# Quarter-tile masks, a first K load in four pieces, zero products at the start, fewer K copies and seven x buffers in a fused attention and mixture kernel

## The chip, the cores and the metric

The kernel runs on 1 core of one Trainium2 chip. The metric is the time of one execution on the device in microseconds (us). Before the change three executions took 289.18, 290.21 and 291.86 us; the median, 290.21 us, is the time to beat. A separate execution was profiled: it took 289.33 us, and its trace spans 287.5 us.

Engines are named as the profile names them: PE does the matrix products (PEld its weight loads), DVE and ACT are the vector and the activation engine, POOL does memory copies and small vector work here, SP issues every DMA transfer.

## The reference, cut to what matters

```
# attention: B=2, H=8, S=768, D=64; window |i-j| < 16 and 24 block summaries
scores_l = scale * q @ k.T ; masked to the window
scores_s = scale * q @ k_sum.T + log(32)      # k_sum: max over blocks of 32 keys
a = softmax(concat(scores_l, scores_s)) ; attn = a @ concat(v, v_sum)   # v_sum: block means
x = attn as [1536, 512]
h = x @ w_in [512, 2048] ; g = h * tanh(softplus(h)) ; y = g @ w_out [2048, 512]
# soft mixture: 8 experts, 4 slots each, D=512, F=1024
logits = y @ phi ; d = softmax over tokens ; slot_input = d.T @ y
slot_out[e] = relu(slot_input[e] @ w1[e]) @ w2[e]
out = softmax over slots(logits) @ slot_out
```

## The kernel before, in words

The 1536 rows are worked through as twelve tiles t = 0..11 of 128 rows, six to a batch. A tile's attention holds 8 heads and two windows of 64 queries. For each window the 120 score columns are 96 window keys and 24 block summaries. PE forms the scores of a tile as 16 products of 64 by 64 by 120 (task `S`, L419), four at a time on the quarters of its array. For t = 0..4 the mask is added on PE by products of `spread_sb` and `mask_sb` that open the accumulation (L414): two products of 128 rows and 480 columns for an inner tile, four on half the columns of the array for an edge tile. For t = 5 and later DVE adds it (`masked`, L434). Then DVE takes the row maximum (`red`, L427), ACT the exponential (L441), DVE or POOL normalizes (`nm`, L456), PE transposes (`AT`, L462), and PE multiplies with V (`AV`, L472) into `x`.

Of `w_in` there are four blocks of 512 columns, fb = 0..3. Each is loaded in two halves of 1 MB through three staging slots (8, 9, 10), and each half is decoded by one ACT pass (L487) and two DVE passes (L488, then L489, which frees the staging slot for the next load). The decoded block is scaled and split in two half-precision planes: the high one by ACT (L518), the low one by DVE (L519, two to a block). Tile 0 uses the decoded block at once in full precision (`H32`, L611); from t = 1 each x is split in two planes too, and `H` is 48 products per tile (L617 to L619). `w_out` comes through the same staging slots. ACT evaluates the activation with `Mish` (L625), which needs another function table than the exponential, so that ACT reloads a table (`ACT_TABLE_LOAD`) at each turn between the two.

The mixture's routing runs beside this, tile by tile (L679 to L770). The 33 expert loads, 16 of `w1` and 17 of `w2` (L848), go into big slots as these come free. The tail is the experts' two products (L915, L967) and the output.

What sets the order: a table `ORDER` of task numbers, `CHOICE` of engines and `SLOT` of buffers. Each engine executes its tasks in that order and stalls on semaphores. All transfers stand in one order on SP, and a transfer that has to wait holds up those behind it.

The names that the change touches: `mask_sb` and `spread_sb` are the mask's two factors; `kb` is K by head, and `kh` is K already cut into windows. In batch 0, K comes as two `kb` loads of 768 KB; DVE reduces each to block maxima (L319), POOL copies these into the K buffer (`kplace`, L372) and cuts the windows of t = 0..5 out of the loaded K (`kwin`, L354 to L360). In batch 1 only t = 6 and 7 are cut on chip; t = 8..11 load `kh`. `x_b` are five x buffers, three in slot 20 and two in slot 21: tile t takes one of slot 21 when t % 5 > 2, that is t = 3, 4, 8, 9. Slot 21 becomes free for an expert load when the last `H` of those tiles is done. `warm` is a new task, `busy` (L664) an old one of the same kind at the end.

Of the kernel before, what the change touches and what calls it, by code (L numbers as in the profile page):

```python
# [21 lines left out]
NT = B * S // 128  # L22
# [78 lines left out]
    ],  # L101
    "POOL": [
        196, 199, 203, 222, 229, 243, 246, 250, 253, 267, 270, 274, 277, 291, 294, 298, 301, 317, 323, 366,
        388, 407, 413, 426, 432, 445, 451,
    ],
}
# [973 lines left out]
```

## Time and profile before

| what | value |
|---|---|
| median of three executions | 290.21 us (289.18 to 291.86) |
| profiled execution | 289.33 us, span 287.5 us |
| PE busy | 268.0 us of the span (93%) |
| DVE, ACT, POOL busy | 195.0, 207.8, 52.2 us |
| moved by DMA | 80.58 MB, mean 280 GB/s |

A busy time says how long an engine had an instruction in work. Start times count from the start of the span. In a timeline row the bracket at the end tells how long the engine stood idle before the row and which instruction let it go on. The clock column (PEclk) is the share of full clock granted to PE; half of it is the lower of its two levels, 1.2 in place of 2.4 GHz.

### The profile page before, as it was taken

To read this page: it belongs to the slowest core of one execution; us is meant where nothing else is said; L and a number is where in the kernel's file an instruction comes from. 1 tells how busy PE (TensorE), PEld (TensorE's weight loads), DVE (VectorE), ACT (ScalarE), POOL (GpSimd) and SP (SyncE) were. 2 spreads that over 40 slices of the span, in tenths; PEclk is the share of its full clock that TensorE was granted. 3 is DMA by queue.
4 is the path that set the end of the run, shared out by engine and by line. 5 is a ranking of instruction groups with operands and counts; after the bars stand their busy time and mean duration, and the time that the engine had idled before them with its cause. 6 is when DMAs were issued, how large, how long until landed. Compare 5 with 4: busy or idle time off the path is not lost.

```text
span 287.5 us, 7828 instructions
## 1 busy us (share of the span) xinstructions
PE 268.0 (93%) x3144; PEld 151.4 (53%) x3144; DVE 195.0 (68%) x460; ACT 207.8 (72%) x488; POOL 52.2 (18%) x91
## 2 busy tenths in 40 slices
PE   0889879999999999999999999999999998999997
PEld 0557445555456564565556545455645743234475
DVE  2489899999999898778659667686523575002352
ACT  1297889979988879999969999899459653003232
POOL 1559225430070531001211111000000010100000
PEclk9997999999999999999999999999999999999999
DMA  7999999599999879999695677989988999999997
GB/s 253 415 358 344 358 339 365 137 335 308 317 246 315 154 107 222 205 241 223 241 192 128 76 222 141 299 157 210 325 317 313 370 388 314 412 423 421 423 346 252
DMA packets 58467, 80.58 MB, mean 280 GB/s; under 512 B 44352, under 2 KB 47936, under 8 KB 53824
## 3 DMA queue, kind: packets, MB, share of 16 engines
q1 hardware_dynamic: 58432, 80.10, 91.3%
q8 instruction: 24, 0.39, 0.5%
q14 instruction: 11, 0.09, 0.1%
HBM read 66.46 MB, written 3.15 MB: 242 GB/s over the span
## 4 chain that ended last, share of the span: by engine, by line
PE 44%; DVE 20%; DMA 16%; ACT 14%; issue 5%; POOL 1%; SPq 0%; DVEq 0%; ACTq 0%; POOLq 0%
PE bank L617 8%; PE bank L619 7%; PE bank L618 7%; DMA slot<-w2b 6%; DVE slot L489 4%; ACT slot L441 4%; DMA slot<-w2a 3%; PE bank L754 2%; ACT slot L625 2%; DMA slot<-kb 2%; DMA slot<-wi 2%; PE bank L472 2%; DVE slot L488 2%; DMA slot<-wo 2%; ACT L625 2%
## 5 line engine op out<-in xcount | busy, mean ns | idle before, releaser
L617 PE MATMUL bank<-slot,slot 128*128 128x512 f16 x176 | 66.9, 380 | 0.7 <-ACT slot L625 0.7
L618 PE MATMUL bank<-slot,slot 128*128 128x512 f16 x176 | 66.7, 379 | 0.0
L619 PE MATMUL bank<-slot,slot 128*128 128x512 f16 x176 | 66.7, 379 | 0.0
L456 POOL TENSOR_TENSOR slot<-slot,sm 128x480 f32<-128x480 f32 x19 | 22.7, 1197 | 91.7 <-DVE sm L452 25.2
L625 ACT ACTIVATE slot<-bank,scal 128x512 f32<-128x512 f32 x44 | 29.2, 687 | 9.8 <-PE bank L619 6.7
L641 DVE SCALAR_TENSOR_TENSOR slot<-slot,sc,slot 128x512 f16<-128x512 f32 x40 | 30.6, 774 | 4.3 <-ACT slot L637 4.0
L619 PEld LDWEIGHTS <-slot 128*128 128x128 f16 x176 | 17.2, 98 | 21.0 <-DVE slot L480 0.3
L255 ACT COPY slot<-bank 120x512 f32<-120x512 f32 (+5 forms) x45 | 17.7, 430 | 14.3 <-PE bank L923 8.3
L617 PEld LDWEIGHTS <-slot 128*128 128x128 f16 x176 | 17.4, 99 | 16.8 <-issue 0.6
L625 ACT ACT_TABLE_LOAD x20 | 25.7, 1283 | 0.8 <-PE bank L619 0.4
L618 PEld LDWEIGHTS <-slot 128*128 128x128 f16 x176 | 17.2, 98 | 16.6 <-issue 1.5
L441 ACT ACTIVATE slot<-slot,sm 128x120 f32<-128x120 f32 x56 | 21.3, 383 | 0.6 <-DVE sm L435 0.5
L441 ACT ACTIVATE slot<-bank,sm 128x120 f32<-128x120 f32 x40 | 13.9, 369 | 10.5 <-POOL sm L431 10.5
L257 DVE COPY slot<-bank 128x256 f32<-128x256 f32 (+3 forms) x30 | 14.4, 513 | 9.8 <-PE bank L462 4.0
L489 DVE SCALAR_TENSOR_TENSOR slot<-slot,slot 128x1024 int32<-128x1024 int32 x16 | 20.4, 1277 | 0.3
L487 ACT ACTIVATE slot<-slot 128x1024 f32<-128x1024 f32 x16 | 18.6, 1172 | 1.8 <-DMA slot<-wi 1.4
L462 PE MATMUL bank<-ident_sb,slot 128*120 128x128 f32 x96 | 14.7, 278 | 2.1 <-POOL slot L456 1.3
L360 POOL COPY slot<-slot 128x192 f32<-128x192 f32 x26 | 13.8, 550 | 12.4 <-DMA slot<-kb 12.3
L967 PE MATMUL bank<-slot,slot 128*32 128x384 f32 (+1 forms) x256 | 15.2, 382 | 0.2 <-DMA slot<-w2b 0.2
L611 PE MATMUL bank<-slot,slot 128*128 128x512 f32 x32 | 15.4, 599 | 0.0
L472 PE MATMUL bank<-slot,slot 120*64 120x64 f32 x384 | 14.6, 233 | 0.5 <-ACT phi_sb L385 0.3
L419 PE MATMUL bank<-slot,slot 64*64 64x120 f32 x384 | 14.2, 289 | 0.6 <-POOL slot L372 0.6
(175 smaller groups left out, 478.4 us busy)
## 6 DMA issues: line engine op xcount, KB each, us to landing
slot<-w SPq DMA_DIRECT2D x16, 1024.0 KB, 5.5
slot<-w2a SPq DMA_DIRECT2D x12, 960.0 KB, 9.0
slot<-wi SPq DMA_DIRECT2D x8, 1024.0 KB, 6.8
slot<-wo SPq DMA_DIRECT2D x8, 1024.0 KB, 6.0
slot<-vh SPq DMA_DIRECT2D x12, 384.0 KB, 5.3
slot<-w2b SPq DMA_DIRECT2D x4, 1024.0 KB, 18.6
slot<-kb SPq DMA_DIRECT2D x4, 768.0 KB, 5.5
slot<-qh SPq DMA_DIRECT2D x12, 256.0 KB, 5.4
```

Of the source, the lines that this page charges most:

```text
L255: sca.copy(dst, src)
L441: sca.activation(A_b[ha.slot][:, hp], src, AF.Exp, bias=m[:, hp:hp + 1], scale=1.0 if late else 0.125, accum_out=m[:, 4 + hp:5 + hp])
L456: (pool if e == "POOL" else vec).tensor_tensor(A_b[ha.slot], A_b[ha.slot], sm_t[hq.slot][:, 4:8].unsqueeze(2).to_broadcast([128, 4, KW]), ...
L472: pe.matmul(banks[hm.slot][64 * r:64 * r + 64, 128 * hp + 64 * w:128 * hp + 64 * w + 64], Vb[i][:, w, c:c + 64], AT_b[hat2[r].slot][0:KW, ...
L487: d = add("ACT", ("dec_a%d" % n,) + name, lambda e: sca.activation(dst(), st(1).bitcast(F32), AF.Prelu, scale=2.0 ** -112, alpha=-(2.0 ** ...
L489: return add("DVE", ("dec_o%d" % n,) + name, lambda e: vec.scalar_tensor_tensor(di(), st(0), 29, di(), op0=ALU.logical_shift_right, op1=AL ...
L611: pe.matmul(banks[hb.slot], xf_b(hx.slot)[:, dc], slots[hw.slot][:, 512 * dc:512 * dc + 512], start=(dc == 0), stop=(dc == 3))
L617: pe.matmul(ps, x[:, 0, dc], w[:, 0, dc], start=(dc == 0), stop=False)
L618: pe.matmul(ps, x[:, 0, dc], w[:, 1, dc], start=False, stop=False)
L619: pe.matmul(ps, x[:, 1, dc], w[:, 0, dc], start=False, stop=(dc == 3))
L625: g_done[t, fb] = [add("ACT", ("mish", t, fb), lambda e, dst=dst, hb=hb, sc=sc: sca.activation(dst(), banks[hb.slot], AF.Mish, scale=sc), ...
L641: d = add("DVE", ("glo", t, fb), lambda e: vec.scalar_tensor_tensor(pv(1), g(), sfb[:, t // TB:t // TB + 1], pv(0), op0=ALU.mult, op1=ALU. ...
```

## The change

1. The masks become 64 by 64 quarters. `mask_sb`, `spread_sb` and a new `bias_sb` (the 24 summary columns) hold the same 64 rows in both halves of the partitions; each is loaded in two transfers. `add_mask` issues for each quarter one product of 96 columns a head and one of 24. A masked tile has eight such products in place of two or four. Every user waits for all six loads (`masks_in`).
2. The first K comes in four loads of 384 KB in place of two, each with its own DVE reduction. K sits in slots 4 and 5, no longer 6 and 7; the decoded blocks 2 and 3 change places with it.
3. `vsum` is zeroed by POOL at the start, and 22 products of zeros (`warm`) are chained on PE.
4. Windows of K are cut on chip for t = 0..3 and 6, 7; t = 4 and 5 load `kh`.
5. There are seven x buffers: slot 21 holds four, for t = 3, 4, 5, 6, 10, 11.
6. `ORDER`, `CHOICE` and `SLOT` are new.

```diff
@@ masks and zero products
-    L_spread = add("DMA", ("ld_spread",), lambda e: dma(out=spread_sb, in_=spread))
-    L_mask = add("DMA", ("ld_mask",), lambda e: dma(out=mask_sb, in_=masks.rearrange("k p n -> p k n")))
+    L_spread, L_mask = None, None
+    for w in range(2):
+        L_spread = add("DMA", ("ld_spread", w), lambda e, w=w: dma(out=spread_sb[HALF[w]].rearrange("p (a m) -> p a m", a=2), in_=spread.rearrange("(a p) m -> p a m", a=2)[:, :, 0:64]), after=[L_spread])
+        L_mask = add("DMA", ("ld_mask", w), lambda e, w=w: dma(out=mask_sb[HALF[w]], in_=masks[:, 0:64].rearrange("k p n -> p k n")), after=[L_mask])
+        L_bias = add("DMA", ("ld_bias", w), lambda e, w=w: dma(out=bias_sb[HALF[w]], in_=masks[0, 64:128, 96:KW]), after=[L_mask])
+    L_mask = join(("masks_in",), [t for t in pl.tasks if t["name"][0] in ("ld_spread", "ld_mask", "ld_bias")])
+    def add_mask(ps, r, w, of, stop):
+        a, at = ps.shape[1], (64 * r, 64 * w)
+        for stat, mov, cols in ((slice(0, 64), mask_sb[HALF[r], of, 0:96], slice(0, 96)), (slice(64, 128), bias_sb[HALF[r]], slice(96, KW))):
+            pe.matmul(ps[HALF[w], :, cols], spread_sb[HALF[r], stat], mov.unsqueeze(1).to_broadcast([64, a, cols.stop - cols.start]), start=cols.start == 0, stop=stop and cols.start > 0, tile_position=at)
+    Z_w = add("POOL", ("fillw",), lambda e: pool.memset(vsum, 0.0))
+    for j in range(22):
+        warm.append(add("PE", ("warm", j), lambda e: pe.matmul(banks[hwarm.slot][:, 0:480], zeros[:, 0:128], zeros[:, 0:480], start=True, stop=True), [warm[-1]], acq=[] if j else [hwarm], use=[hwarm] if j else []))
@@ scores
-                for rows, of in () if late else [(slice(0, 128), 1)] if kind == 1 else [(slice(0, 64), min(kind, 1)), (slice(64, 128), max(kind, 1))]:
-                    pe.matmul(ps[rows], spread_sb[:, rows], mask_sb[:, of].unsqueeze(1).to_broadcast([128, 4, KW]), start=True, stop=False)
+                for w, of in () if late else [(0, min(kind, 1)), (1, max(kind, 1))]:
+                    add_mask(ps, r, w, of, False)
@@ K
-        hk = [Hold(stage if b else wslot[2 + i]) for i in range(2)]
+        hk = [Hold(stage if b else wslot[i]) for i in range(2)]
+                k4.append(add("DMA", ("ld_kq", i, h), lambda e, i=i, h=h: dma(out=slots[hk[i].slot][:, 768 * h:768 * h + 768], in_=kb[b, :, 2 * i + h]), acq=[] if h else [hk[i]], use=[hk[i]] if h else [], after=k4[-1:]))
+                ks.append(add("DVE", ("ksumq", i, h), lambda e, i=i, h=h: vec.tensor_reduce(ksum[:, 2 * i + h], slots[hk[i].slot][:, 768 * h:768 * h + 768].rearrange("p (n s) -> p n s", n=NB), axis=AX.X, op=ALU.max), [k4[-1]], use=[hk[i]]))
-            for t in range(2, TB):
-                K_in[t] = windows
+            K_in[2] = K_in[3] = windows
@@ x
-... x_b = [...] for s, i in ((20, 0), (20, 1), (20, 2), (21, 0), (21, 1))]
+... x_b = [...] for s, i in ((20, 0), (20, 1), (20, 2), (21, 0), (21, 1), (21, 2), (21, 3))]
+    X_TWO = (3, 4, 5, 6, 10, 11)
-        hx, hm = Hold(xring2 if t % 5 > 2 else xring), Hold(mring)
+        hx, hm = Hold(xring2 if t in X_TWO else xring), Hold(mring)
-    give([21], [H_last[t, fb] for t in range(NT) if t % 5 > 2 for fb in range(4)])
+    give([21], [H_last[t, fb] for t in X_TWO for fb in range(4)])
...
```

The first transfers on SP, before (slots are counted from 72, so slot_78 is slot 6):

```order
L314 DMA slot_78<-kb 128x1536
L314 DMA slot_79<-kb 128x1536
L264 DMA spread_sb<-spread 128x128
L265 DMA mask_sb<-masks 128x3x120
L400 DMA slot_88<-qh 128x512
L262 DMA ident_sb<-ident 128x128
L263 DMA bmean_sb<-bmean 128x144
```

and now:

```order
L269 DMA spread_sb<-spread 64x2x64
L270 DMA mask_sb<-masks 64x3x120 x2
L338 DMA slot_76<-kb 128x768 x2
L338 DMA slot_77<-kb 128x768
L271 DMA bias_sb<-masks 64x24
L338 DMA slot_77<-kb 128x768
L269 DMA spread_sb<-spread 64x2x64
L271 DMA bias_sb<-masks 64x24
L265 DMA ident_sb<-ident 128x128
L425 DMA slot_88<-qh 128x512
```

Three small loads now stand ahead of the first K load, and the second halves of `spread` and `bias` stand behind the last.

DVE in the stretch that decodes `w_in` (sm are the small scale buffers; slots 11, 12 and 4 or 6 hold decoded blocks, slots 0 and 3 planes, slots 8 to 10 staging), before:

```order
L519 SCALAR_TENSOR_TENSOR slot3_75<-slot5_77,sm7_113,slot3_75 128x1024
L488 TENSOR_SCALAR slot12_84<-slot12_84 128x1024
L489 SCALAR_TENSOR_TENSOR slot12_84<-slot10_82,slot12_84 128x1024
L519 SCALAR_TENSOR_TENSOR slot0_72<-slot11_83,sm0_106,slot0_72 128x1024
L427 TENSOR_REDUCE sm1_107<-bank4_65 128x4
L488 TENSOR_SCALAR slot12_84<-slot12_84 128x1024
L489 SCALAR_TENSOR_TENSOR slot12_84<-slot8_80,slot12_84 128x1024
```

and now:

```order
L544 SCALAR_TENSOR_TENSOR slot3_75<-slot7_79,sm7_114,slot3_75 128x1024
L322 TENSOR_REDUCE bnd_115<-bank6_67 128x1
L513 TENSOR_SCALAR slot6_78<-slot6_78 128x1024
L307 TENSOR_REDUCE sm0_107<-bnd_115 128x1
L514 SCALAR_TENSOR_TENSOR slot6_78<-slot9_81,slot6_78 128x1024
L300 TENSOR_REDUCE sm0_107<-bank7_68 128x1
L302 TENSOR_SCALAR sm0_107<-sm0_107 128x1
L305 TENSOR_SCALAR sm0_107<-sm0_107 128x1
L306 TENSOR_SCALAR scal_106<-sm0_107 128x1
L513 TENSOR_SCALAR slot12_84<-slot12_84 128x1024
```

The first low plane (L519 before, L544 now) has moved ahead of the decode of block 2's first half (L488 and L489 before, L513 and L514 now); before, it stood behind that decode.

The expert loads around the last DMA transposes on SP (slot_93 is slot 21, slot_88 is slot 16), before:

```order
L848 DMA slot11_83<-w1 128x2048
L848 DMA slot12_84<-w1 128x2048
L644 DMA_TRANSPOSE slot22_94<-slot10_82 128x8x128 x4
L644 DMA_TRANSPOSE gx_t_125<-slot13_85 128x8x128
L848 DMA slot21_93<-w1 128x2048
L644 DMA_TRANSPOSE slot22_94<-slot13_85 128x8x128 x3
L848 DMA slot16_88<-w1 128x2048
```

and now:

```order
L873 DMA slot18_90<-w1 128x2048
L669 DMA_TRANSPOSE gx_t_126<-slot15_87 128x8x128
L669 DMA_TRANSPOSE slot22_94<-slot10_82 128x8x128 x4
L873 DMA slot16_88<-w1 128x2048
L669 DMA_TRANSPOSE gx_t_126<-slot13_85 128x8x128
L669 DMA_TRANSPOSE slot22_94<-slot13_85 128x8x128 x3
L873 DMA slot17_89<-w1 128x2048
```

The load into slot 21 has left its place; it now stands as the last but one of the 16 `w1` loads. The load into slot 16 stands where it stood.

On ACT the order before holds 41 `ACT_TABLE_LOAD`, as the trace does; the order now holds 33. Six of the tasks L637 and a few evacuations changed places between ACT and DVE.

## Rows read from the trace of the kernel before

**Rows 1.** Windows of four stages: engine busy us (instructions), clock, DMA share, GB/s.

```profile
0.00:9.40 9.40, 1.02 (x5) 0.32 (x5) 3.51 (x2) 1.28 (x1) 2.70 (x16) 1.00 0.84 288
15.80:50.50 34.70, 30.40 (x291) 18.99 (x282) 33.05 (x73) 30.22 (x70) 16.68 (x24) 0.95 0.98 351
50.50:230.00 179.50, 175.97 (x2126) 101.32 (x2124) 136.93 (x319) 157.19 (x349) 27.09 (x39) 1.00 0.89 232
245.80:273.30 27.50, 27.16 (x298) 10.61 (x291) 4.54 (x8) 5.07 (x16) 1.06 (x1) 1.00 1.01 422
```

**Rows 2.** Timeline of the start: start us, us, engine, line, operation [idle before].

```profile
0.74 0.89 SPq L314 DMA_DIRECT2D slot<-kb  x2
1.67 0.42 SPq L264 DMA_DIRECT2D spread_sb<-spread  x1
2.14 0.56 SPq L265 DMA_DIRECT2D mask_sb<-masks  x1
...
7.26 1.75 DVE L319 TENSOR_REDUCE slot<-slot 128x48 f32<-128x1536 f32 x1 [0.22 <-DMA slot<-kb]
...
9.39 2.08 PE L419 MATMUL bank<-slot,slot 64*64 64x120 f32 x32 [0.59 <-POOL slot L372]
...
15.84 1.16 ACT L487 ACTIVATE slot<-slot 128x1024 f32<-128x1024 f32 x1 [0.22 <-DMA slot<-wi]
```

**Rows 3.** Windows of PE alone: busy us (instructions), clock, DMA share, GB/s.

```profile
14.96:16.00 1.04, 1.04 (x34) 1.00 1.12 435
18.00:19.80 1.80, 0.65 (x4) 1.00 1.10 314
21.00:22.50 1.50, 1.50 (x34) 0.57 0.98 377
22.50:24.40 1.90, 1.90 (x36) 0.50 0.94 354
```

**Rows 4.** Timeline of DVE, 22 to 50 us.

```profile
22.56 1.89 DVE L489 SCALAR_TENSOR_TENSOR slot<-slot,slot 128x1024 int32<-128x1024 int32 x1
...
31.73 0.69 DVE L488 TENSOR_SCALAR slot<-slot 128x1024 int32<-128x1024 int32 x1 [0.47 <-ACT slot L487]
...
49.10 1.27 DVE L519 SCALAR_TENSOR_TENSOR slot<-slot,sm,slot 128x1024 f16<-128x1024 f32 x1
```

**Rows 5.** All executions of L488, L489, L519: duration ns min/median/max, first and last start.

```profile
L488 DVE TENSOR_SCALAR slot<-slot x16: 662/684/1470, 17.7 to 80.1; 128x1024 int32<-128x1024 int32 x16
L489 DVE SCALAR_TENSOR_TENSOR slot<-slot,slot x16: 1195/1224/1891, 19.7 to 82.3; 128x1024 int32<-128x1024 int32 x16
L519 DVE SCALAR_TENSOR_TENSOR slot<-slot,sm,slot x8: 1275/1280/2009, 34.8 to 77.6; 128x1024 f16<-128x1024 f32 x8
```

**Rows 6.** Timeline of PE: the longest stall of the decode, the first half-precision H product.

```profile
39.19 0.63 PE L300 MATMUL bank<-slot 128*128 128x128 bf16 x8 [1.84 <-DVE slot L489]
...
50.56 0.38 PE L617 MATMUL bank<-slot,slot 128*128 128x512 f16 x1
...
54.45 0.57 PE L414 MATMUL bank<-mask_sb,spread_sb 128*128 128x480 bf16 x2
```

**Rows 7.** Groups by shape: xcount | busy us, mean ns | idle before, releaser.

```profile
L414 PE MATMUL bank<-mask_sb,spread_sb 128*128 128x480 bf16 x8 | 2.4, 367 | 0.1
L625 ACT ACT_TABLE_LOAD x20 | 25.7, 1283 | 0.8 <-PE bank L619 0.4
```

**Rows 8.** Waits of PE: us in total, times, longest.

```profile
PE bank L617 <- ACT slot L625: 0.7, 2, 0.4
...
PE bank L730 <- ACT eT L718: 0.6, 1, 0.6
```

**Rows 9.** DMA issues: xcount, KB each, median us to landing.

```profile
slot<-w SPq DMA_DIRECT2D x16, 1024.0 KB, 5.5
...
slot<-wi SPq DMA_DIRECT2D x8, 1024.0 KB, 6.8
...
slot<-kh SPq DMA_DIRECT2D x4, 384.0 KB, 4.7
```

More of the change, by code (lines that the diff above doesn't have):

```diff
@@ L245, in local_summary_attention_mish_soft_moe @@
     wslot = [Ring([4 + k]) for k in range(4)]
-    aring, atring, xring, xring2, gtring, gpring = Ring(range(2)), Ring(range(2)), Ring(range(3)), Ring([3, 4]), Ring(range(5)), Ring(range(4))
+    aring, atring, xring, xring2, gtring, gpring = Ring(range(2)), Ring(range(2)), Ring(range(3)), Ring([3, 4, 5, 6]), Ring(range(5)), Ring(range(4))
     smring, expring, gextra, g23, g8, once = Ring(range(8)), Ring(), Ring(), Ring(), Ring(), Ring()
@@ L308, in batch @@
     def batch(b):
-        hk = [Hold(stage if b else wslot[2 + i]) for i in range(2)]
+        hk = [Hold(stage if b else wslot[i]) for i in range(2)]
         hv = [Hold(stage) for i in range(2)] if b else [homed(15, gring), homed(23, g23)]
         hs = Hold(smring)
-        lk, lv, ks, vm = [], [], [], []
+        lk, lv, ks, vm, k4 = [], [], [], [], []
         for i in range(2):
-            lk.append(add("DMA", ("ld_kb", b, i), lambda e, i=i: dma(out=slots[hk[i].slot][:, 0:1536], in_=kb[b, :, 2 * i:2 * i + 2].rearrange("p h s -> p (h s)")), acq=[hk[i]]))
+            if b:
+                lk.append(add("DMA", ("ld_kb", b, i), lambda e, i=i: dma(out=slots[hk[i].slot][:, 0:1536], in_=kb[b, :, 2 * i:2 * i + 2].rearrange("p h s -> p (h s)")), acq=[hk[i]]))
+                continue
+            for h in range(2):
+                k4.append(add("DMA", ("ld_kq", i, h), lambda e, i=i, h=h: dma(out=slots[hk[i].slot][:, 768 * h:768 * h + 768], in_=kb[b, :, 2 * i + h]), acq=[] if h else [hk[i]], use=[hk[i]] if h else [], after=k4[-1:]))
+                ks.append(add("DVE", ("ksumq", i, h), lambda e, i=i, h=h: vec.tensor_reduce(ksum[:, 2 * i + h], slots[hk[i].slot][:, 768 * h:768 * h + 768].rearrange("p (n s) -> p n s", n=NB), axis=AX.X, op=ALU.max), [k4[-1]], use=[hk[i]]))
+            lk.append(join(("kb_in", i), k4[-2:]))
         for i in range(2):
-            lv.append(add("DMA", ("ld_vn", b, i), lambda e, i=i: dma(out=slots[hv[i].slot][:, 0:1536], in_=vn[b, :, 3 * i:3 * i + 3].rearrange("p h s -> p (h s)")), acq=[hv[i]], after=lv[-1:]))
+            lv.append(add("DMA", ("ld_vn", b, i), lambda e, i=i: dma(out=slots[hv[i].slot][:, 0:1536], in_=vn[b, :, 3 * i:3 * i + 3].rearrange("p h s -> p (h s)")), acq=[hv[i]]))
         old_k = [] if b == 0 else [KP[0], KP[1], KP[2], KP[3]]
         for i in range(2):
-            ks.append(add("DVE", ("ksum", b, i), lambda e, i=i: vec.tensor_reduce(ksum[:, 2 * i:2 * i + 2], slots[hk[i].slot][:, 0:1536].rearrange("p (h n s) -> p h n s", h=2, n=NB), axis=AX.X, op=ALU.max), [lk[i]] + old_k, use=[hk[i]]))
+            b and ks.append(add("DVE", ("ksum", b, i), lambda e, i=i: vec.tensor_reduce(ksum[:, 2 * i:2 * i + 2], slots[hk[i].slot][:, 0:1536].rearrange("p (h n s) -> p h n s", h=2, n=NB), axis=AX.X, op=ALU.max), [lk[i]] + old_k, use=[hk[i]]))
             if b:
@@ L338, in batch @@
             V_read.extend([vs] + vm)
-        vc = add("ACT", ("vgather", b), gather, [vs] + old_v, use=[hb])
+        vc = add("ACT", ("vgather", b), gather, [vs] + (old_v or [warm[-1]]), use=[hb])
         if b == 0:
@@ L383, in near_mask, with mm @@
         hm = Hold(mring)
-        q = add("PE", ("near_mm",), lambda e: pe.matmul(banks[hm.slot][:, 0:KW], spread_sb, mask_sb[:, 1], start=True, stop=True), [L_spread, L_mask] + W2_parts, acq=[hm])
+        def mm(e):
+            for w in range(2):
+                add_mask(banks[hm.slot][:, 0:KW].rearrange("p (a k) -> p a k", a=1), 0, w, 1, True)
+        q = add("PE", ("near_m4",), mm, [L_spread, L_mask] + W2_parts, acq=[hm])
         near_done.append(add("ACT", ("near_ev",), lambda e: sca.mul(near, banks[hm.slot][:, 0:KW], 0.125), [q], use=[hm]))
@@ L391, in mm @@
             for n in range(2):
-                for rows, of in ((slice(0, 64), n), (slice(64, 128), n + 1)):
-                    pe.matmul(banks[hm.slot][rows, KW * n:KW * n + KW], spread_sb[:, rows], mask_sb[:, of], start=True, stop=True)
-        q = add("PE", ("edge_mm",), mm, [L_spread, L_mask], acq=[hm])
+                for w in range(2):
+                    add_mask(banks[hm.slot][:, KW * n:KW * n + KW].rearrange("p (a k) -> p a k", a=1), 0, w, n + w, True)
+        q = add("PE", ("edge_m4",), mm, [L_spread, L_mask], acq=[hm])
         edge_done.append(add("ACT", ("edge_ev",), lambda e: sca.mul(edge_t.rearrange("p n k -> p (n k)"), banks[hm.slot][:, 0:2 * KW], 0.125), [q], use=[hm]))
@@ L419, in sc @@
                         pe.matmul(banks[hs2[r].slot][64 * w:64 * w + 64, KW * hp:KW * hp + KW], Qb[i][d, 4 * w + hp], Kb[i][d, :, 4 * w + hp], start=late, stop=(late or hp == 3), tile_position=(64 * r, 64 * w))
-        s = add("PE", ("S" + ("" if late else "m" if kind == 1 else "e"), t), sc, [lq, *lks, kp[0], kp[1], L_spread, L_mask] + [last_S[0]], acq=hs2)
+        s = add("PE", ("S" + ("" if late else "m4" if kind == 1 else "e4"), t), sc, [lq, *lks, kp[0], kp[1], L_spread, L_mask] + [last_S[0]], acq=hs2)
         last_S[0] = S_t[t] = s
```

16 lines of the change are left out of this document (9 added, 7 removed), and 161 rows, old and new, of tables (CHOICE, ORDER, SLOT).

## The prediction, made before the result was known

> **What bounds the kernel now.** I read the windows by stage first, because 93% busy for PE is an average over five different limits [rows 1]. Until 9.4 us PE is idle but for 1.0 us: it waits for data. From 15.8 to 50.5 DVE is busy 33.05 of 34.7 us and PE idles 4.3: `w_in` is being decoded, and DVE sets the pace. From 50.5 to 230 PE is busy 175.97 of 179.5; all that can be won there by better order is the 3.53 us it idles. From 245.8 to 273.3 DMA is at 1.01 of its capacity and 422 GB/s: the tail cannot end before the last expert weights land, and these can start only as slots come free behind PE's work before 245.8. So a microsecond gained by PE before 230 is kept to the end, and one gained by DVE before 50 is kept as far as PE waits for DVE.
>
> Second, the timeline of the start [rows 2]. The first K load is issued at 0.74 us, the second reduction starts at 7.26 when the second load has landed, ends at 9.01, and the scores of tile 0 start at 9.39. The first `w_in` half lets ACT go on at 15.84. Third, the timeline of DVE [rows 4] with the spread of its three long operations [rows 5], and PE beside it [rows 6]: the longest stall of PE there, 1.84 us, ends when an L489 ends.
>
> **The head: taken as 0.** Ahead of the first K load now stand one `spread` and two `mask` issues, by their rows 0.42 + 2 × 0.56 = 1.5 us [rows 2]. The bytes of K are the same, so I put the last quarter of K at 7.26 + 1.5 = 8.8. Its reduction is half as long (1.75 / 2 = 0.88), so the block maxima are ready at 9.7, not 9.01; with the 0.38 that `kplace` takes up to 9.39, tile 0 could start at 10.1. The masks come later too: every user waits for all six loads, and the second `spread` and `bias` stand behind the last K quarter, at about 9.0. Behind them PE has the edge mask, four zero products and tile 0's eight mask products, about 2 us, so that the scores start at 10.1 to 11.5. Before, they took 2.08 us, where tile 1's took 1.04 [rows 2, 3]. At the faster pace they end at 11.1 to 12.5, before at 11.47: between −0.4 and +1.0.
>
> What this is worth later is decided by the `w_in` loads. The first landed at 15.84 and is now put at up to 17.2. But in the new order its L488 and L489 follow each other at once. I walked DVE's new order with 0.66 for L488, 1.2 for L489, 1.2 for L519, the medians less the overlap of neighbours [rows 5], and 6 us from issue to landing, under the median of 6.8 [rows 9]. The third half is decoded at 28.2, where it was before. So the late K is made up within the decode; nearest bounds −0.6 (the second ring load released earlier) and +1.4 (the whole delay of the first half handed on).
>
> **The decode: −1.2.** The same walk, further on: DVE used to idle 0.47 us at 31.73 for a half that was not yet there [rows 4]; the first L519 now stands in that place, and the reductions of the scores of t = 3 come earlier. In the walk DVE has four L519 and all that stands ahead of them done at 49.2. Before, the fourth of them ended at 49.10 + 1.27 = 50.4 [rows 4], at equal numbers of other work. The gain is one L519. PE's first H product would move from 50.56 [rows 6] to 49.4. PE's own stall of 1.84 us at 39.19 goes, because more `H32` products stand ready, but in the walk a wait of about 2.8 us for block 1's second half appears at 39.5, so I count it as moved. Bounds: 0 (a new stall) and −2.0 (the slow L489 of 1.89, an L488 of 1.47 and an L519 of 2.01 are partly POOL's doing, and POOL has fewer copies).
>
> **The masks: +0.3.** One product of 480 columns lasts 0.367 us, two in a row 0.57, so a further one costs 0.20 [rows 6, 7]. The eight new products are four of 384 columns and four of 96. The two of a quarter go one after the other; only the next quarter's first can run beside a quarter's second. That is 3 × 384 + 480 = 1632 columns, 0.68 us in place of 0.40: +0.28 for each of t = 1 to 4. Only t = 4 stands where PE has no slack [rows 1, 6]. All four dearer and an edge tile 0.12 cheaper gives +1.0; all quarters abreast gives −0.20 for an inner tile, −0.8 for four. The Trainium skill, "TensorEngine Tiling (Array Packing)", Key Properties, says that different tiles of the array work independently and in parallel. By it the masks would cost 480 columns a tile and the sum would be 0.5 lower; no row here shows this shape.
>
> **The later waits of PE: −1.3.** The order drops 8 of 41 table loads, each 1.283 us [rows 7], 10.3 us of ACT, all after about 90 us, and gives ACT six more L637 in return. PE's waits that end with ACT between 50 and 230 are 0.7 and 0.6 us [rows 8]; I take these two. Bounds 0 and −3.5, all of PE's idle time there [rows 1].
>
> **At nothing.** The copies of `kwin` that go (t = 4, 5) lie on POOL, busy 16.68 of 34.7 us [rows 1]; nobody waits for them. Two more `kh` loads, 0.79 MB, land in 4.7 us [rows 9] and are issued long before their tiles; uncovered they cost 0.79 MB / 422 GB/s = 1.9 us of DMA. Seven x buffers: I found no wait of PE or ACT for a free x, so they can only help the order. Slot 21 is handed back after tile 11 and not after tile 9; the load into slot 16 stands in its place on SP, so the same six loads precede the last transposes.
>
> **Sum:** 0 − 1.2 + 0.3 − 1.3 = −2.2. Against the profiled execution, 289.33, that is 287.1. The median of the runs is 0.9 above it, so I forecast **288.0 us**.
>
> **Rivals.**
>
> *The clock.* The scores of tile 0 took 2.08 us against 1.04 [rows 2, 3], and the stretch from 21.0 to 24.4 had clocks of 0.57 and 0.50, that is the lower level, after PE had been busy for only 0.65 us between 18.0 and 19.8 [rows 3]. If the zero products keep the upper level, PE saves 1.04 there and 1.5 × 0.43 + 1.9 × 0.5 = 1.6 here. If PE and not DVE were the bound in the head, that is 2.6 more: 285.4. For it: tile 0's x waits for PE's `AV`. Against: DVE is busy 33.05 of 34.7 [rows 1], and a PE that is faster waits longer. The Trainium skill, "TensorE: Matmul & The Clock Gate", says in its Part 1 that the array's clock is low by default and activity releases it. By that rule this rival is what the zero products are good for; the trace agrees as to the fall after an idle stretch. Chance 0.13.
>
> *All later waits go.* ACT is relieved so far that PE hardly waits between 50 and 230: 2.2 us more than I took, 285.8. Against: the rows name ACT for only 1.3 of the 3.5 us [rows 8]. Chance 0.15.
>
> *The change does not do what it says.* K quarters that wait behind the masks land later than the halves did, the zero products delay tile 0, and the gain of the decode is eaten: about 290.2. Chance 0.17.
>
> *Slower.* The tail. From 245.8 us DMA is full [rows 1], so every megabyte that leaves the stretch before it comes out behind the end. The load into slot 21, 1024 KB [rows 9], moves to the end of `w1`. If the load into slot 16 that takes its place waits for tile 10's `AV`, and this comes late in the new order, no load stands in the gap: 1.05 MB / 422 GB/s = 2.5 us, 292.7 with nothing gained, 293 and more if the loads behind it on SP wait as well. It decides once slot 16 is free later than slot 21 was. Chance 0.13.
>
> **How the numbers follow.** The forecast has 0.42. Three runs of this kernel differ by 0.9%, so 1% (2.9 us) is about what can be told from no change: under 287.3 is faster, above 293.1 slower. Faster takes the clock, the later waits and a quarter of the forecast's own spread: 0.13 + 0.15 + 0.10 = 0.38. Slower takes most of the last rival, 0.10. The rest, 0.52, is no change. The range goes from 284.2 (the two gains, with 1.2 us for their bounds) to 292.8 (the tail).
>
> **What would show it.** Right, if in the new profile the fourth low plane of `w_in` is done by about 49 us and the first half-precision H product starts at 49 to 50; if the first decode on ACT starts at 16.5 to 17.5; if PE idles about 2 us, not 3.5, between there and the last routing; if the last `w2` weights land about 2 us earlier. The masks are wrong if the eight products take 0.4 us or less. The forecast is wrong if the first H product stands where it stood, or if SP waits for slot 16 before the last transposes.

## The result, and the profile after

The change made the kernel slower: 294.68 us, the median of 4 runs (293.32 to 295.16), against 289.78 for 4 runs of the kernel before, a ratio of 1.0124 with a 95% interval of 1.0078 to 1.0170. Here and below, medians are of all executions, while a ratio leaves out those slowed by a disturbance from outside the kernel and is not the quotient of the two medians (1.017 here). The forecast was 288.0 with a range of 284.2 to 292.8, so both the time and the sign were wrong. The profiled execution took 295.16 us with a span of 293.4, 5.9 more than before. That is more than the 3.6 us that the ratio gives or the 4.9 between the medians; what follows explains this one pair of executions.

First the stages of the start, where the forecast had a zero. Windows of the changed kernel, columns as in [rows 1]:

```profile
core 0: us, PE busy (x) PEld busy (x) DVE busy (x) ACT busy (x) POOL busy (x), PEclk, DMA share, GB/s
2.50:5.00 2.50, 2.50 (x8) 0.89 (x6) 0.00 (x0) 0.00 (x0) 0.00 (x0) 1.00 0.57 68
5.00:7.50 2.50, 0.71 (x3) 0.18 (x2) 0.51 (x1) 0.00 (x0) 0.00 (x0) 1.00 1.00 356
7.50:10.00 2.50, 0.00 (x0) 0.00 (x0) 2.37 (x4) 0.00 (x0) 1.48 (x6) 1.00 1.00 336
10.00:12.50 2.50, 2.18 (x15) 0.84 (x18) 0.91 (x1) 0.37 (x1) 1.63 (x7) 1.00 0.95 319
```

The first of these stretches in the kernel before:

```profile
2.50:5.00 2.50, 0.00 (x0) 0.00 (x0) 0.00 (x0) 0.00 (x0) 0.00 (x0) 1.00 0.91 344
```

Between 2.5 and 5 us 68 GB/s move now, where it was 344; over the first 9.4 us it is 188, where it was 288 [rows 1]. The reader is to see that DMA, which sets the pace of the start, begins 2.5 us late and is at 319 to 356 afterwards (before: 376 to 412 from 5 to 10). What SP issued meanwhile, by its timeline in the changed kernel (start, us, line, transfer; x is the number of transfers in a row):

```profile
0.73 0.74 SPq L269 DMA_DIRECT2D spread_sb<-spread  x1
1.53 1.25 SPq L270 DMA_DIRECT2D mask_sb<-masks  x2
2.82 1.55 SPq L338 DMA_DIRECT2D slot<-kb  x3
4.41 0.50 SPq L271 DMA_DIRECT2D bias_sb<-masks  x1
4.96 0.59 SPq L338 DMA_DIRECT2D slot<-kb  x1
5.58 0.60 SPq L269 DMA_DIRECT2D spread_sb<-spread  x1
6.23 0.60 SPq L271 DMA_DIRECT2D bias_sb<-masks  x1
6.88 0.58 SPq L265 DMA_DIRECT2D ident_sb<-ident  x1
7.51 0.43 SPq L425 DMA_DIRECT2D slot<-qh  x1
7.98 0.43 SPq L342 DMA_DIRECT2D slot<-vn  x1
8.90 0.33 SPq L425 DMA_DIRECT2D slot<-qh  x1
9.28 0.43 SPq L342 DMA_DIRECT2D slot<-vn  x1
9.95 0.79 SPq L521 DMA_DIRECT2D slot<-wi  x1
```

The first `w_in` load is the sixteenth transfer and is issued at 9.95 us; before it was the eleventh:

```profile
7.62 0.43 SPq L496 DMA_DIRECT2D slot<-wi  x1
```

Six transfers of 3 to 45 KB take 0.50 to 0.74 us of SP each. Now the places that the prediction named, from the timelines of ACT, DVE and PE in the changed kernel (the first decode on ACT, tile 2's mask products and first scores, the fourth low plane, the first half-precision H product, and a stall at 99 us):

```profile
19.30 1.15 ACT L512 ACTIVATE slot<-slot 128x1024 f32<-128x1024 f32 x1 [1.17 <-DMA slot<-wi]
...
24.15 0.37 PE L279 MATMUL bank<-mask_sb,spread_sb 64*64 64x384 bf16 x4
24.34 0.22 PE L279 MATMUL bank<-bias_sb,spread_sb 64*64 64x96 bf16 x4
24.38 1.02 PE L444 MATMUL bank<-slot,slot 64*64 64x120 f32 x32
...
50.37 1.27 DVE L544 SCALAR_TENSOR_TENSOR slot<-slot,sm,slot 128x1024 f16<-128x1024 f32 x1
...
53.83 0.38 PE L642 MATMUL bank<-slot,slot 128*128 128x512 f16 x1
...
99.12 0.34 PE L704 MATMUL bank<-slot,slot 128*32 128x128 f16 x12
101.61 1.96 PE L354 MATMUL bank<-slot,bmean_sb 128*24 128x128 f32 x48 [2.15 <-ACT slot L466]
...
104.08 0.63 PE L642 MATMUL bank<-slot,slot 128*128 128x512 f16 x1
```

The first decode stands at 19.30 (15.84 before [rows 2]) and waits for its load; the first H product at 53.83 (50.56 [rows 6]). So the head's +3.5 stands at the first H product as +3.3. Counted at every 24th H product, PE stays 1.8 to 4.3 us behind up to the 121st of 528 (+3.1 there). Then PE waits 2.15 us for the block means of V of batch 1. The row names ACT's L466, but that writes a slot that L354 doesn't read; the second V load, issued at 92.60, had landed 8.9 us later, at 101.5. Until 105.8 products then run slower (0.63 us for an H product, 0.38 elsewhere; the granted clock of 100 to 105 is 0.75, a mean of the two levels). The 145th H product is 6.4 us late, the last one 6.0, the end 5.9 (3.4 to 7.9 between, since the two orders place other work differently among the products). Two losses, then: about 3.3 before 54 us and about 3 at 99 us.

### The profile page after: what moved, and what is told of

The parts are those of the page before. It is cut to its first block, busy times and chain, and to the rows that moved or that the text cites. A ratio compares the mean times of both kernels' runs of the same rounds, so it can differ in the third digit from the quotient of the medians.

```text
span 293.4 us, 7935 instructions
## 1 busy us (share of the span) xinstructions
PE 274.5 (94%) x3201; PEld 153.9 (52%) x3201; DVE 194.7 (66%) x460; ACT 201.7 (69%) x482; POOL 49.9 (17%) x82
## 4 chain that ended last, share of the span: by engine, by line
PE 56%; DVE 21%; ACT 8%; DMA 8%; issue 4%; SPq 2%; ACTq 0%; DVEq 0%
PE bank L642 8%; PE bank L643 7%; PE bank L644 7%; DMA slot<-wi 7%; PE bank L992 5%; PE bank L940 5%; DVE slot L514 4%; DVE slot L666 4%; PE bank L497 3%; ACT slot L466 2%; DVE slot L544 2%; PE bank L444 2%; PE bank L779 2%; PE bank L704 2%; PE bank L487 2%
## 5 line engine op out<-in xcount | busy, mean ns | idle before, releaser
L481 POOL TENSOR_TENSOR slot<-slot,sm 128x480 f32<-128x480 f32 x20 | 23.5, 1175 | 115.8 <-DVE sm L477 93.8
L666 DVE SCALAR_TENSOR_TENSOR slot<-slot,sc,slot 128x512 f16<-128x512 f32 x40 | 33.2, 841 | 3.5 <-ACT slot L662 3.1
L258 ACT COPY slot<-bank 128x256 f32<-128x256 f32 (+5 forms) x42 | 17.0, 428 | 21.7 <-PE bank L973 10.0
L260 DVE COPY slot<-bank 128x256 f32<-128x256 f32 (+5 forms) x34 | 16.5, 500 | 8.5 <-PE bank L918 3.1
L466 ACT ACTIVATE slot<-slot,sm 128x120 f32<-128x120 f32 x56 | 21.3, 383 | 0.7 <-DVE sm L460 0.7
L514 DVE SCALAR_TENSOR_TENSOR slot<-slot,slot 128x1024 int32<-128x1024 int32 x16 | 20.5, 1283 | 0.1
L636 PE MATMUL bank<-slot,slot 128*128 128x512 f32 x32 | 17.1, 659 | 1.0 <-DVE slot L514 1.0
L466 ACT ACTIVATE slot<-bank,sm 128x120 f32<-128x120 f32 x40 | 13.8, 364 | 4.9 <-DVE sm L456 4.1
L992 PE MATMUL bank<-slot,slot 128*32 128x384 f32 (+1 forms) x256 | 15.8, 382 | 0.0
L662 ACT ACTIVATE slot<-slot,sc 128x512 f16<-128x512 f32 x22 | 15.6, 719 | 0.3
L497 PEld LDWEIGHTS bank<-slot,slot 120*64 120x64 f32 x384 | 12.6, 138 | 3.8 <-issue 2.8
```

Source lines behind the costliest of these rows:

```text
L466: sca.activation(A_b[ha.slot][:, hp], src, AF.Exp, bias=m[:, hp:hp + 1], scale=1.0 if late else 0.125, accum_out=m[:, 4 + hp:5 + hp])
L481: (pool if e == "POOL" else vec).tensor_tensor(A_b[ha.slot], A_b[ha.slot], sm_t[hq.slot][:, 4:8].unsqueeze(2).to_broadcast([128, 4, KW]), ...
L497: pe.matmul(banks[hm.slot][64 * r:64 * r + 64, 128 * hp + 64 * w:128 * hp + 64 * w + 64], Vb[i][:, w, c:c + 64], AT_b[hat2[r].slot][0:KW, ...
L514: return add("DVE", ("dec_o%d" % n,) + name, lambda e: vec.scalar_tensor_tensor(di(), st(0), 29, di(), op0=ALU.logical_shift_right, op1=AL ...
L666: d = add("DVE", ("glo", t, fb), lambda e: vec.scalar_tensor_tensor(pv(1), g(), sfb[:, t // TB:t // TB + 1], pv(0), op0=ALU.mult, op1=ALU. ...
L992: pe.matmul(banks[hh.slot][32 * j:32 * j + 32, 0:nc_], hM(fc // 4)[:, j, 32 * e_:32 * e_ + 32], w[:, o:o + nc_], start=(e_ == 0 and fc < 4 ...
```

## The experiments

All times are medians; ratios are against the kernel before on the same chip. "First H" is the start of the first half-precision H product in the profiled execution, 50.56 before and 53.83 after the change. One execution is not exact in it: f1 and g1 below have the same order up to there and differ by 1.4 us, e1 and e4 by 1.1. So smaller differences in first H are not read, and runs of different sets are compared by their ratios.

**First set: place of K, zero products, place of the block means.** The edits, in the table of numbers unless said otherwise:

```diff
 e1   K quarter loads 35, 37, 40, 42 ahead of spread and mask loads (2, 3, 6)
 e2   - pe.matmul(banks[hwarm.slot][:, 0:480], zeros[:, 0:128], ...)   # all 22
 e3   five H tasks 693, 701, 694, 695, 696 ahead of vmean (365)
 e4   e1 and e3
```

> The changed kernel with one thing moved: the four quarter loads of K stand first on SP, ahead of spread and masks; all else is in the same order. Theory 1 (late loads): the changed kernel moves next to nothing until 5 us, since three small loads stand ahead of K, and everything up to the first half-precision H product (53.83 us, before 50.56) is late by that. Then the first w_in half is decoded on ACT at about 17 us and not at 19.30, the first H product starts at 51 to 52, and the time falls by 2.0 to 2.8 us against the changed kernel, to about 292.2. Rival A (the six extra issues on SP and not their place are what costs): K's maxima come earlier, but the first w_in load is still issued at about 10 us; first H product at 53 or later, time falls by less than 1 us. Rival B (the zero products or the order hold tile 0 back): no change within 0.5 us.

Measured: 293.54 us, 1.0111 [1.0062, 1.0160], first H 53.74. By the ratios that is 0.4 us less than the changed kernel, which is within the noise. Theory 1 falls, rival A stands. The timeline of SP in that run:

```profile
0.73 1.82 SPq L341 DMA_DIRECT2D slot<-kb  x4
2.60 0.73 SPq L272 DMA_DIRECT2D spread_sb<-spread  x1
3.37 1.25 SPq L273 DMA_DIRECT2D mask_sb<-masks  x2
4.66 0.61 SPq L274 DMA_DIRECT2D bias_sb<-masks  x1
5.32 0.60 SPq L272 DMA_DIRECT2D spread_sb<-spread  x1
5.96 0.60 SPq L274 DMA_DIRECT2D bias_sb<-masks  x1
7.04 0.34 SPq L268 DMA_DIRECT2D ident_sb<-ident  x1
8.40 0.33 SPq L428 DMA_DIRECT2D slot<-qh  x1
...
10.20 0.43 SPq L524 DMA_DIRECT2D slot<-wi  x1
```

And two of its windows, columns as above, DMA share and GB/s last:

```profile
5.00:7.50 2.50, 0.50 (x2) 0.00 (x0) 1.55 (x3) 0.00 (x0) 1.48 (x6) 1.00 0.94 291
7.50:10.00 2.50, 0.83 (x9) 0.70 (x10) 1.45 (x2) 0.11 (x1) 1.32 (x6) 1.00 0.34 53
```

K is there early: its reductions start at 4.19, 7.04 and 8.40. But the six small loads take 3.8 us of SP between 2.60 and 6.56, and then SP stands. The eleventh transfer (`ident`) leaves at 7.04 and the twelfth at 8.40, which is when DVE starts on the third and fourth K quarter (landed at 7.02 and 8.38): this program lets a transfer go only when the one eight before it has landed. So DMA ran dry, 53 GB/s from 7.5 to 10, and `w_in` was issued at 10.20, no sooner than before the edit.

> The changed kernel without its 22 products of zeros on PE (left out, their result is never read); all else the same. Theory 1 (late loads): PE is not what is waited for in the head, so the first H product stays at 53.5 to 54 and the time within 0.7 us of the changed kernel. Rival B (zero products hold tile 0 back: four of them, 0.40 us each, stand between the edge mask and tile 0's scores): scores 1.2 to 1.6 us earlier, and 1 to 1.5 us less time. Rival C (they pay, by keeping PE's clock at the upper level): the scores and the block means run at the lower level, and the time rises by 0.5 to 1.5 us.

Measured: 294.62 us, 1.0102 [1.0055, 1.0148], first H 54.24. No difference that can be told: the zero products neither hold tile 0 back nor pay. The scores of tile 0 start at 12.82 in this run and at 12.81 with the zero products; here they wait 1.92 us for the load of q.

> The changed kernel with five tasks of PE moved: 15 H products of tile 4 (0.216 us each, 3.2 us) stand ahead of the block means of V of batch 1 and not behind them. Theory 2 (a new wait in the order): in the changed kernel PE waits 2.15 us at 99.5 for the second V load of batch 1 and then runs at a lower clock until 105.8; the number of H products done falls back there from +3.1 to +6.4 us against the kernel before. With the products ahead the wait is covered: no wait of more than 0.5 us there, no fall of the clock, and 2.5 to 4 us less time, about 291.5. Rival D (the wait only moves: the block means gate tile 6, and what they gate comes late instead): a new wait of 1 to 2 us between 100 and 125, time within 1 us of the changed kernel. Rival E (the end is set by the transfers of the tail and not by PE there): PE gains but the time stays within 1 us.

Measured: 294.45 us, 1.0142 [1.0105, 1.0179]. The 145th H product came at 100.12 and not at 105.36, but by the 169th all but 1 us of that was gone. The timeline of PE in that run shows where:

```profile
102.81 1.51 PE L357 MATMUL bank<-slot,bmean_sb 128*24 128x128 f32 x48
...
106.19 1.06 PE L490 MATMUL bank<-ident_sb,slot 128*120 128x128 f32 x8 [1.46 <-DVE slot L484]
...
108.36 1.04 PE L447 MATMUL bank<-slot,slot 64*64 64x120 f32 x28 [0.47 <-DVE slot L263]
```

The same 15 products had been covering the transposes of tile 5; moved forward, they uncover them. Rival D holds: the wait moves along the change of batches.

> Both moves at once: K first on SP, and the block means of batch 1 behind the 15 H products. Theories 1 and 2 together: the gains add up, 4.5 to 6.5 us less than the changed kernel, 288 to 290, level with the kernel before or a little faster. If the two are one thing (the late head causes the later wait): no more gain than the better of the two alone, 291 to 292. If neither: 294 to 295.

Measured: 294.89 us, 1.0126 [1.0090, 1.0162]. Nothing adds up; both moves treat what is late, not why.

**Second set: the number of loads.** The constants are laid out as [128, 512] (128 columns of spread, 360 of masks, 24 of bias), and one load fetches them. In e5 the V load takes the staging slot and the place of the K load, and K those of V. b1 is the kernel before with the new mask products:

```diff
 f1   e1, and
-  6 x dma(spread_sb[HALF[w]] | mask_sb[HALF[w]] | bias_sb[HALF[w]], ...)
+  dma(out=const_sb, in_=masks)        # [128, 512] bf16, 128 KB
 e5   ld_kb/1/0 (slot 8) <-> ld_vn/1/0 (slot 9); their readers on POOL, DVE later
 g1   f1 and e5
 b1   kernel before, add_mask() of the change, its six loads behind the K loads
```

> The changed kernel with K first on SP and the six loads of spread, masks and bias replaced by one load of 128 KB of the same values, laid out ready by the constants; all else the same. Theory 1b (the number of transfers in flight): in the run with K first alone DMA was down to 9 to 139 GB/s between 7 and 10 us, because SP stood at the ninth transfer until an earlier one had landed, and w_in was issued at 10.2 us as in the changed kernel. With five issues fewer w_in is issued at 7 to 8 us, the first decode on ACT starts at 15.5 to 17 (19.30), the first half-precision H product at 50 to 51.5 (53.83), and the time falls by 2 to 3.5 us against the changed kernel, to about 291.8. Rival E (what is won in the head is lost again at the change of batches, 99 to 115 us, or in the tail): the head as said, but the time within 1 us of the changed kernel, 294 to 295.

Measured: 289.73 us, 0.9962 [0.9934, 0.9991], first decode 15.96, first H 49.66. Its timeline of SP:

```profile
0.73 1.82 SPq L341 DMA_DIRECT2D slot<-kb  x4
2.60 0.43 SPq L272 DMA_DIRECT2D const_sb<-masks  x1
3.07 0.43 SPq L268 DMA_DIRECT2D ident_sb<-ident  x1
3.54 0.43 SPq L428 DMA_DIRECT2D slot<-qh  x1
4.02 0.43 SPq L345 DMA_DIRECT2D slot<-vn  x1
4.49 0.43 SPq L428 DMA_DIRECT2D slot<-qh  x1
5.09 0.33 SPq L345 DMA_DIRECT2D slot<-vn  x1
6.05 0.33 SPq L524 DMA_DIRECT2D slot<-wi  x1
```

The issue of `w_in` moved from 10.20 to 6.05 by taking five transfers away, with the same bytes; by the ratios the time fell by 4.3 us. The gain is not all of the earlier issue: `w_in` leaves 1.57 us sooner than in the kernel before, yet its decode starts 0.12 later (15.96 and 15.84), behind the same bytes of K, q and V. What came back is DMA's work in the first 9.4 us, 282 GB/s (188 in the changed kernel, 288 before). The second loss went as well, untouched by the edit. The waits of PE in this run have, for the block means:

```profile
PE bank L357 <- DMA slot<-vn: 0.8, 1, 0.8
```

That is 0.80 us and not 2.15. Against this run the changed kernel is 4.2 us behind from the first to the 121st H product, and 6.9 to 7.2 from the 145th to the last: all of the second loss falls at this wait. In the other runs whose head is late and which leave the wait in its place it is 1.44 to 2.57 us (e1, e2, f4), in those with the head cured 0.80 to 0.99 (f2, f3, h1). So the stall at 99 us came from the late head, on top of a shorter one that the new order has by itself: its second V load of batch 1 lands at 95.95 in f1, where before both had landed by 89.3 and the block means started at 91.5 without a wait.

> The changed kernel, with the first K load and the second V load of batch 1 exchanged on SP (and their staging slots), and three tasks on POOL and DVE that read that K put later accordingly. Theory 2 (the V load is late and PE waits for it): both V loads have landed by 97 us, the block means of batch 1 start at 99.5 without a wait, the clock stays at its upper level through 105, and 2.5 to 4 us are won, about 291.5. Rival D (the change of batches is a chain and the wait only moves along it): the scores of tile 6 wait for K instead, a stall of 1.5 us or more between 103 and 112, time within 1 us of the changed kernel.

Measured: 294.42 us, 1.0098 [1.0066, 1.0131]: no gain on the changed kernel that can be told, as rival D has it. Its profiled execution took 297.61 us, 3.2 over the median, so its trace is not read, and where the wait went is not shown here.

> Both: K first with one load of constants, and V before K in batch 1. Theories 1b and 2: the gains add up, first H product at 50 to 51.5, no stall at 99 to 105, 288 to 290 us. Rivals D and E: 293 to 295.

Measured: 289.70 us, 0.9965 [0.9938, 0.9992], first H 51.08, the same time as f1. The wait for the V load is gone, and the scores at 104.67 us wait 1.1 us for a copy of POOL in its place: with the head cured too, the exchange only moves the wait.

> The kernel before with its own order and one part of the change alone: the masks as products on quarter tiles, with their six loads issued behind the two K loads, where the two loads of masks stood. Theory 1b (four more transfers in flight hold up what follows them): the first w_in load is issued at 9 to 10.5 us (7.62), the first half-precision H product starts 1.5 to 3 us later than 50.56, and the time rises by 1.5 to 3 us against the kernel before, less up to 1 us that the masks win (0.23 us ahead of a tile's scores and not 0.50, as the changed kernel's trace shows). Rival F (the loads of the masks cost nothing behind K, only ahead of it): first H product at 50 to 50.8, time 0 to 1 us below the kernel before.

Measured: 292.87 us, 1.0086 [1.0052, 1.0119]; `w_in` issued at 9.88, first H 52.60, +2.04. Every 24th H product after it is 1.99 to 2.08 late, and the last one 1.99: in this run the late head is handed on one to one. It fits theory 1b, but the third set showed that the quarter products cost something in this order with one load too, so these 2 us cannot be put down to the loads.

**Third set: place, zero products and size apart.**

```diff
 f2   one constant load, left ahead of K (no e1)
 f3   f1 without the 22 zero products
 f4   f1 with the load cut by columns: 128, 120, 120, 120, 12, 12
 b2   b1 with one constant load
```

> The changed kernel with the six loads of spread, masks and bias replaced by one of 128 KB, and this one left where the first of them stands, ahead of K; nothing else is moved. Theory 1b (the number of transfers decides, not their place): first w_in load issued at 6 to 7.5 us, first half-precision H product at 49.5 to 51.5, time within 0.7 us of the kernel with K first and one constant load (289.7). Theory 1 (the place ahead of K costs too): K lands 0.5 us later and the first H product stands 1 us or more behind that kernel's 49.66; time 291 or more.

Measured: 288.92 us, 0.9962 [0.9930, 0.9994], `w_in` issued at 6.29, first H 49.83. The place ahead of K costs nothing that can be measured. Against the changed kernel this is the plainest pair, one load for six and nothing moved: 4.7 us less by the ratios.

> The kernel with K first and one constant load, without the 22 products of zeros on PE (left out; their result is never read). Rival B (four of them stand between the edge mask and tile 0's scores): tile 0's scores start up to 1.2 us earlier, time up to 1 us less. Rival C (they keep PE's clock up): the granted clock below 25 us falls, and the time rises by 0.5 to 2 us. Theory: DVE and the loads set the pace of the head, so the first H product is within 0.7 us of 49.66 and the time within 0.7 us of 289.7.

Measured: 289.52 us, 0.9966 [0.9932, 0.9999]. First H stood at 51.42, 1.1 past what was expected but within what differs between executions, and the time is level with f1: the zero products are worth nothing here either.

> The kernel with K first and one constant load, with that load cut into six by columns, all 128 partitions and no more bytes than before. It parts two things that six loads cost: SP's time to issue them and the landings that SP waits for. Both together (the run with K first alone) put the first w_in load at 10.2 us, one load at 6.05. If it is only SP's time, five more issues of 0.43 to 0.6 us put it at 8.2 to 9, the first H product at 51 to 52 and the time at 291 to 292. If the limit of transfers in flight costs as well, SP waits for landings for 1 us or more, w_in is issued at 9.5 to 10.5, first H product at 52 to 54 and the time is 292.5 to 294.5.

Measured: 292.08 us, 1.0044 [1.0013, 1.0074], first H 54.20. From its timeline of SP:

```profile
2.60 3.03 SPq L272 DMA_DIRECT2D const_sb<-masks  x6
...
9.10 0.44 SPq L524 DMA_DIRECT2D slot<-wi  x1
```

Issuing the six took 3.03 us with a wait of 0.3 us for a landing of K in it, and SP waited 0.6 and 0.7 us more for K's landings before `w_in`. It lies between the two expectations: by the ratios, cutting one load in six, byte for byte the same, costs about 2.4 us, by issue time and by waits. With the number of transfers the size of their packets changes too (1057 packets under 512 bytes in the first 20 us, 235 in f1), and this pair does not part the two. It also leaves 1.9 us open between this run and e1, whose six loads take half the partitions each and longer to issue (0.60 to 0.73 us each, where these take 0.33 to 0.46); the two intervals overlap, so that part is not shown.

> The kernel before with its own order and the masks as products on quarter tiles, all their values in one load in the place of the two loads of spread and masks. Against the run with six loads (first H product 52.60, 292.9 us) the delay of the head should be gone: w_in issued at 7 to 7.7 us, first H product at 49.8 to 50.6, time 0.3 to 1.3 us below the kernel before (290.7) by what the masks win, 0.25 us for each of up to four tiles. If the quarter products themselves cost (my forecast of 0.28 us more for each tile): 0.3 to 1.3 us above it.

Measured: 293.79 us, 1.0110 [1.0064, 1.0157], a miss. `w_in` was issued at 7.18 as expected, yet first H stood at 54.59. The timeline of PE in that run:

```profile
39.66 0.77 PE L306 MATMUL bank<-slot 128*128 128x128 bf16 x8 [2.05 <-DVE slot L495]
41.54 1.97 PE L478 MATMUL bank<-slot,slot 120*64 120x64 f32 x32 [1.11 <-DMA slot<-vh]
43.44 1.11 PE L468 MATMUL bank<-ident_sb,slot 128*120 128x128 f32 x4
44.34 3.12 PE L617 MATMUL bank<-slot,slot 128*128 128x512 f32 x4
```

Two waits stand close together, and the granted clock of 40 to 45 is 0.50: four products in single precision take 3.12 us (1.88 before). The clock is at its lower level there. The wait on `vh` is for the V load of tile 1, issued at 31.90 and landed 9.5 us later (7.6 before). Against b1 (1.0086) one load in place of six won nothing in the old order that can be told.

**Fourth set: what the masks themselves are worth.**

```diff
 b3   kernel before, full masks, spread and masks in one load [128, 488]
 b4   b2, ld_v/1 (216) ahead of ld_wi1/1/0/0 (53)
 b5   b4, ld_v/2 (240) ahead of ld_wo1/1/0/0 (133)
 h1   f2 with the mask products of the kernel before (full array, 480 columns)
```

> The kernel before, its masks as they were (products on the full array), but spread and masks in one load of 122 KB and not in two. If the quarter products cost in the old order: this is level with the kernel before, 289.5 to 291, and 3 us under the quarter products with one load (293.8). If the one load costs, by moving every later transfer: 292.5 to 294.5.

Measured: 290.73 us, 0.9991 [0.9960, 1.0021]: in the old order the one load in place of two costs nothing and wins nothing that can be told.

> The kernel before with quarter products and one load, and the V load of tile 1 two w_in loads earlier on SP. If the late V load makes the loss (PE waits 1.1 us for it at 41.5 and then runs at the lower clock until about 46): no wait of AV for V, first half-precision H product at 50 to 52 and not 54.59, time 290 to 291.5. If not: 293 to 294.5, with the first H product at 53.5 or later.

Measured: 292.20 us, 1.0053 [1.0018, 1.0088], first H 51.70. That wait for V is gone and about half of the loss with it, but at 58.1 AV waits 1.16 us for the V load of tile 2, behind two `w_out` loads, and PE runs at 0.63 us a product until 63.6.

> The kernel before with quarter products and one load, with the V loads of tiles 1 and 2 both earlier on SP (tile 2's ahead of two w_out loads). If late V loads are all that the quarter products cost in the old order, by PE's wait and the lower clock after it: no wait of AV for V, and 290 to 291, level with the kernel before. If the products cost something else: 291.7 or more.

Measured: 292.26 us, 1.0068 [1.0027, 1.0108], first H 53.20, and no wait of AV for V. So late V loads are not all of it. That the quarter products cost something in the old order is shown: b2 and b3 differ in little else, by about 3.5 us of the ratios, and 1.5 to 2 us are left over the kernel before with the V loads earlier (b4, b5). By what is open.

> The changed kernel's order with one load ahead of K, as in the run of 288.9 us, but with the masks as products on the full array, as in the kernel before: the quarter products are the only difference. Their worth is 0.25 us ahead of a tile's scores (0.23 and 0.50), in five tiles. If they are on the path of the head: first H product 0.5 to 1.2 us later than 49.83 and 0.5 to 1.2 us more time, 289.4 to 290.1. If PE has slack there: within 0.5 us of 288.9.

Measured: 289.13 us, 0.9931 [0.9899, 0.9964], first H 50.47. With the old mask products and one load the new order is level with f2, and it is the version that is surest to beat the kernel before. In the new order the quarter products win nothing on the path, and cost nothing that can be told.

## Why the prediction was wrong, step by step

**The head, taken as 0, is the step that failed.** It named the right place and counted the wrong thing. It asked when K would land, and put three issues ahead of it at 1.5 us; they took 2.0 (0.74 and 1.25), and the last K quarter was reduced at 10.9, not 9.7. That alone is what e1 undid, and it was worth nothing that can be told. What it left out is that all six loads and two more K pieces stand ahead of `w_in`: 15 transfers where there were 10. Each holds SP for 0.33 to 0.74 us and holds one of eight places until it lands, and meanwhile DMA moved 188 GB/s where it had moved 288. The forecast had tile 0's scores at 10.1 to 11.5 and the first `w_in` half at 17.2 at the latest; the scores started at 12.81 and the decode at 19.30. "The late K is made up within the decode" failed with it: the third half was decoded at 31.4, not 28.2, because the decode followed the loads. The worst case that I allowed, +1.4, was less than half of the +3.5.

**A late head is not only handed on.** In the new order runs with first H at most 0.9 us later than before ended their H products at −1.1 to +1.3 (f1, f2, f3, g1, h1); those 2.1 or more late ended at +3.7 or more (e1, e2, e3, e4, f4 and the change itself), 1.4 to 1.8 times as late. The forecast had no term for the change of batches, where the new order has less room.

**The decode, −1.2: not borne out in the form it was given.** In f1, where the first decode is 0.1 us later than before, the fourth low plane ended at 47.27, 3.1 us earlier than before and earlier than the 49.2 of the forecast; in the changed kernel it ended at 51.6. But the forecast let the first H product follow that plane as it did before, 0.2 us behind it. In f1 it stands 2.4 us behind, at the end of work that keeps PE busy without a break from 43.0 on. So first H came only 0.9 earlier, which is within what differs between executions, and no gain is shown: PE is busy for 170.59 us between the first and the last H product, 169.69 before, so as much work has moved behind the first H product as it came earlier.

**The masks, +0.3: wrong in sign, and of no weight in the new order.** I took the two products of a quarter as a chain and only neighbours as abreast. The rows at 24.15 to 24.38 show all eight within 0.23 us ahead of the scores. In h1, at the same place, the two full products need 0.50 (timeline of PE):

```profile
21.50 0.57 PE L276 MATMUL bank<-const_sb 128*128 128x480 bf16 x2
22.00 1.05 PE L440 MATMUL bank<-slot,slot 64*64 64x120 f32 x32
```

The Trainium skill, "TensorEngine Tiling (Array Packing)", Key Properties, says that different tiles can run matmuls in parallel; the trace agrees. A tile's products came out at −0.27, near the lower bound of −0.20 and not at +0.28. But h1 against f2 shows that 0.27 us a tile is not on the path. The cost of the same products in the old order (b2 against b3) had no term at all, and stays open.

**The later waits, −1.3: near in size with the head cured, in the changed kernel not there.** Between the first and the last H product PE idles 2.42 us in f1, 3.53 before and 3.69 in the changed kernel. The eight table loads are gone, and of the two waits on ACT, 0.7 and 0.6 us, one of 0.2 is left. But others went too (1.3 us on POOL), and waits of 1.0 and 0.8 us stand elsewhere (a copy on DVE and the V load). So the −1.1 agrees with the forecast in part by luck, and that the table loads make it is not shown. With the head cured, all the rest of the change is worth about 1.1 us by the ratios (f1, f2), half of the −2.2 forecast.

**The rivals.** The clock had nothing in it: e2 and f3 leave the zero products out at no cost. The slower rival named the tail; DMA had no gap there (a share of 0.99 to 1.02 from 229 to 280 us), and the tail started 6 us later. "The change doesn't do what it says" named K behind the masks, which was the lesser part (0.4 us by the ratio of e1); its time, 290.2, was too low because it left the queue out.

## What to carry to other kernels

Count the transfers ahead of the one that starts the pipeline, not only their bytes: each costs its issue and a place in a queue of limited depth. In the changed kernel a 3 KB load held SP for 0.50 and 0.60 us and a 768 KB load for 0.43, and each took one of eight places. Lay constants out so that one load brings them; here that was worth 4.7 us in the new order (f2) and nothing that can be told in the old one (b1, b2), so measure it where it stands. A kernel whose order is a table tuned at one timing has room in some places and none in others, so a delay at the start came out 1.4 to 1.8 times as long at the last H product here, and curing the later stall moved it while curing the start removed most of it.

## What was not expected of the hardware

- Loads of 3 KB (`bias`) took a median of 3.9 to 4.3 us from issue to landing beside K, those of 384 KB 4.6 to 4.7. In every trace the plain loads on SP landed in the order of their issue, so a small one waits for what stands ahead: in the changed kernel the first `bias` landed 0.18 us after the K piece before it. Where less stood ahead, 64 and 72 KB took 1.8 and 1.9 us (b1) and 128 KB, the first of all, 2.2 (f2). The Trainium skill, "DMA: Bandwidth & Descriptors", Anatomy of one DMA, gives a fixed part of about 2.0 us for a transfer of another issuing path; these three are near it.
- After a wait of 2.15 us PE needed 4.2 us to be back at its pace (101.6 to 105.8); after two waits of 2.05 and 1.11 us the granted clock was 0.50, the lower level, for 40 to 45.
- What DMA moved from 12 to 50 us differed between profiled executions, 331 to 363 GB/s in eleven of them. Part of that is the runs' different orders; with the same order up to there it was 353 and 343 (f1, g1), 347 and 357 (e1, e4). The executions of one kernel spread by about 1% either way; that the rate of DMA makes this spread is not shown.
